# Seven joined pairs of steps for five in the last block of an RWKV and dense kernel, with the late forms ahead of the adds

## The chip, the cores and the metric

One core of a Trainium2 chip runs the kernel. The metric is the device time of one execution in microseconds (us). A core has a matrix engine (TensorE; PE in the profile, its weight loads PEld), a vector engine (VectorE, DVE), a scalar engine (ScalarE, ACT), GpSimd (POOL), and queues for transfers (SP). Each engine runs its own instructions in the order in which they were written and waits for the others by semaphores.

## The reference

An attention block of the RWKV kind runs over 768 tokens of 4 x 8 heads of 48 channels. Its output, 3072 tokens of 384 channels, goes through two dense layers with h - tanh(h) between them.

```python
    for t in range(S):
        kt, vt, rt, wt = (k[:, :, t], v[:, :, t], r[:, :, t], w[:, :, t])
        cur = np.einsum('bhd,bhe->bhde', u[None] * kt, vt)
        y[:, :, t] = np.einsum('bhd,bhde->bhe', rt, state + cur)
        state = wt[:, :, :, None] * state + np.einsum('bhd,bhe->bhde', kt, vt)
...
    h = x @ w_in          # (3072, 384) @ (384, 2048)
    g = h - np.tanh(h)
    return (g @ w_out).astype(np.float32)
```

## The kernel before

**Blocks and steps.** The 3072 tokens are cut into eight blocks of 384 tokens (blocks 0 to 7). While the dense layers of one block run, the attention of the next block is prepared beside them. The dense part of a block has 16 steps f, one for each 128 of the 2048 hidden channels. A plain step (`first`, L885) makes h = w_in[f] x in three matmuls of 384 columns, one for each 128 input channels, in the PSUM bank hp. ScalarE copies h out (L890) and squares it twice (L972, L973), VectorE makes g from it (L893), and ScalarE watches the size of h (L977, "junk").

**The fifteen products.** Two steps make a pair q = f // 2. The second layer of a pair takes 15 products of 128x128 where the plain way takes 18 (class `Fewer`, L1085). Products use g itself or sums of parts of g, the forms of g, which VectorE makes in five additions (`form_g`, L1006). The first two are made right behind g. The other three (numbers 4, 6 and 8) are late: they are kept in `held_back`, then `forming`, and, where steps are joined, `carried`. Products 0 to 11 are added over the pairs in three banks acc in two parts of six: the first part two steps after the pair's last g, the second part one step later. Products 12 to 14, the late products (`others`), are added for four pairs at a time in a scratch bank att. Form 8 is read by the fifth of the second part's six products, which the trace shows as the group `acc<-w_sb,g` behind eight rows of `acc<-forms,g`. At the end of a block ScalarE takes acc out (L1097) and VectorE sums it into the output (`SUMS`, L1120), in the steps of the next block.

**Joined pairs.** Only the last block has no attention to prepare beside it. There the first layer of five of its eight pairs (1 to 5, `TWOS`) is joined too (class `Twos`): two steps by two halves of the tokens by three parts of the input channels, 12 products of 192 columns, are had from 11 (L944). They need sums of weights (`weight_forms`, L916) and of tokens (`token_forms`, L925), made ahead, which lie in tiles that the attention no longer needs (k, r, post). The 11 products go to the two scratch tiles e0 and e1 of two banks each, and to hp. ScalarE copies the first product out (L945), and VectorE makes the two h from it in four adds (L954): the first reads e0, the other three e1.

**Order.** The order of each engine is the order in which the program is written, step by step. For each step the list `ops` sets VectorE's order: `rest` (the products that make g), `formed` (an early form of g), `forming` or `carried` (late ones), `outs` (the four adds), `spare` (sums of the block before, and forms of weights and tokens), `behind` (others). `between` takes two lists in turn. Tiles keep their bank as long as someone reads them; the order of waits shows that a scratch tile att of two banks is handed over as a whole.

**The end.** After pair 5 come four plain steps (12 to 15). Their g goes into the output directly (`added`, L1063), behind a check of the sizes of h.

Of the kernel before, what the change touches and what calls it, by code (L numbers as in the profile page):

```python
# [37 lines left out]
F32 = mybir.dt.float32  # L38
# [13 lines left out]
P = 128  # L52
# [4 lines left out]
NCP = NCH // 2  # L57
NPAIR = H // 2
# [7 lines left out]
DM = H * D  # L66
# [5 lines left out]
HB = NB // 2  # L72
# [3 lines left out]
LAST = 6  # L76
# [37 lines left out]
SUMS = (("sub", (15, 6, 10), (0, 0, 6)), ("sub", (2, 2, 5), (3, 5, 3)),  # L114
        ("add", (6, 7, 13), (1, 7, 1)), ("add", (7, 9, 14), (5, 9, 11)),
        ("sub", (10, 10, 14), (5, 5, 6)), ("add", (11, 12, 11), (10, 2, 10)),
        ("sub", (14, 4, 14), (11, 3, 11)), ("add", (2, 8, 13), (10, 5, 10)),
        ("add", (13, 4, 13), (2, 2, 15)), ("add", (8, 8, 12), (4, 4, 12)),
        ("add", (0, 4, 0), (11, 2, 11)), ("sub", (14, 14, 1)))
PLACES = ((8, 10, 0), (2, 5, 13), (11, 7, 14))  # L120
TWOS = range(1, 6)


SLIGHT = 2.0 ** -6
# [4 lines left out]
def kernel(  # L129
# [170 lines left out]
    def scratch(ps):  # L300
        return ps.tile([P, 2, BANK], F32, name="att", tag="att")
# [594 lines left out]
    class Twos:  # L896
# [3 lines left out]
        def __init__(self):  # L900
            def spare(name):
                return inp.tile([P, 2 * HALF], F32, name=name, tag=name)

            n = (TWOS[-1] + 1 - TWOS[0]) * P
            k, r, post = spare("k"), spare("r"), spare("post")
            self.forms = [t[:, a:a + n].rearrange("p (j c) -> p j c", c=P)
                          for t, a in ((k, 0), (k, n), (r, 0), (r, n), (post, 0))]
            self.turned = [post[:, n + a * HB:n + (a + 1) * HB] for a in range(4)]
            self.to = None

        def weight_forms(self):

            at = w_in_sb[:, 2 * TWOS[0]:2 * TWOS[-1] + 2].rearrange("p (j two) k c -> p j two k c", two=2)
            (a11, a12, a13), (a21, a22, a23) = ([at[:, :, i, k] for k in range(KC)] for i in range(2))
            s1, s2, s3, s4, s5 = self.forms
            return [lambda op=op, of=of: nc.vector.tensor_tensor(out=of[0], in0=of[1], in1=of[2], op=OPS[op])  # L916
                    for op, *of in (("add", s1, a21, a22), ("sub", s3, a11, a21), ("sub", s2, s1, a11),
                                    ("sub", s5, a13, a23), ("sub", s4, a12, s2))]

        def token_forms(self, xs):  # L920

# [6 lines left out]
        def begin(self, ps, j):  # L928

            if self.to is None:  # L930
                self.to = [inp.tile([P, 2 * HALF], F32, name=name, tag=name)[:, 0:8 * HB].rearrange(
                    "p (n t) -> p n t", t=HB) for name in ("pre", "w")]
            h, k = self.to[j % 2], j - TWOS[0]
            e0, e1 = ps.both[(ps.n + 1) % 2], ps.both[ps.n % 2]
            (a11, a12, a13), (_, a22, a23) = ([w_in_sb[:, 2 * j + i, k] for k in range(KC)] for i in range(2))
            s1, s2, s3, s4, s5 = (t[:, k] for t in self.forms)
            t1, t2, t3, t4 = self.turned
            (b11, _), (b21, b22), (b31, b32) = self.first, self.second, self.third
            for to, *of in ((hp[:, 0:HB], (a11, b11)), (e0[:, 0, 0:HB], (a12, b21), (a13, b31)),
                            (e0[:, 0, HB:NB], (s2, t2)), (e1[:, 0, 0:HB], (s3, t3)),  # L940
                            (e1[:, 0, HB:NB], (s1, t1), (a23, b32)), (e1[:, 1, 0:HB], (s4, b22), (s5, b32)),
                            (e1[:, 1, HB:NB], (a22, t4), (a23, b31))):
                for n, (lhs, rhs) in enumerate(of):
                    nc.tensor.matmul(to, lhsT=lhs, rhs=rhs, start=n == 0, stop=n + 1 == len(of))  # L944
            nc.scalar.copy(out=h[:, 7], in_=hp[:, 0:HB])  # L945

            def both(t):
                return t.rearrange("p (n t) -> p n t", t=HB)

            def twice(t):  # L950
                return t.unsqueeze(1).to_broadcast([P, 2, HB])

            self.h = [h[:, n:n + 2].rearrange("p n t -> p (n t)") for n in (0, 2)]
            return [lambda of=of: nc.vector.tensor_tensor(out=of[0], in0=of[1], in1=of[2], op=ALU.add)  # L954
                    for of in ((h[:, 0:5:4], twice(h[:, 7]), both(e0[:, 0, 0:NB])),
                               (h[:, 5:7], twice(h[:, 4]), both(e1[:, 0, 0:NB])),
                               (h[:, 1], h[:, 6], e1[:, 1, 0:HB]),
                               (h[:, 2:4], twice(h[:, 5]), e1[:, 1::-1, HB:NB]))]
# [112 lines left out]
    class Fewer:  # L1071
# [24 lines left out]
        def scaled(self, to, src):  # L1096
            nc.scalar.activation(out=to, in_=src, func=AF.Copy, scale=1.0 / UPSCALE)  # L1097

        def others(self, ps, qs):
            if qs[0] % 4 == 0:  # L1100
                self.apart = scratch(ps)[:, 0]
            for q in qs:
                for n in range(MAIN, len(PRODUCTS)):
                    at = (n - MAIN) * P
                    self.product(self.apart[:, at:at + P], q, n, q % 4 == 0 and n == MAIN,
                                 q in (3, self.pairs - 1))
            if qs[-1] == 3:
                self.half = dense.tile([P, DM], F32, name="o", tag="o", bufs=2)
                self.scaled(self.half, self.apart[:, 0:DM])
# [224 lines left out]
    for i, blk in enumerate(blocks):  # L1334
# [9 lines left out]
        for f in range(NF):  # L1344
# [24 lines left out]
            else:  # L1369
                ahead_of_h, square = [], []  # L1370
            some = ({4: (0, 2), 6: (2, 4), 8: (4, 6), 9: (6, 8), 14: (8, len(SUMS))} if later else
                    {4: (0, 1), 5: (1, 2), 6: (2, 3), 7: (3, 4), 8: (4, 5), 9: (5, 9), 10: (9, 10),
                     11: (10, len(SUMS))}).get(f) if summed else None
            spare = summed[0].sum(*some) if some else []
            if now > 1:
                for of, names in ((later, before.get(f, ())), (after, ahead.get(f, ()))):
# [1 line left out]
                              if of and not name.startswith("bound")]  # L1378
            if i:
                spare += [lambda n=n: form_w(n, 4 if f < 12 else 6, 2) for n in formed_w.get(f, ())]  # L1380
            if i == blocks_n - 2 and f == 13:
                twos = Twos()
            if i == blocks_n - 2 and f in (13, 14):
                spare += twos.weight_forms()[(0, 3)[f - 13]:(3, 5)[f - 13]]
            if not later and f == 1:
                spare += twos.token_forms(here)
            adding = []
            if fewer and second and f > 2 * LAST + 1:
                adding = fewer.sum(*((0, 6) if f % 2 == 0 else (6, len(SUMS))))
            if not now:  # L1390
                ops = square + converting(pieces, 2)
            elif now == 1:
                ops = rest + late + square + converting(pieces, 3)
            elif not i:
                ops = extra + square + (rest + behind + spare if f < 7 else rest[:1] + behind + spare + rest[1:])
            elif outs:
                ops = (between(rest, carried[:1]) + outs[:1] + carried[1:] + formed + outs[1:2] + spare + outs[2:])
                carried = []
            elif joined:
                ops, carried = forming[:1] + between(rest + formed, spare), forming[1:]  # L1400
            elif carried:
                ops, carried = between(rest + formed, carried + behind + spare), []
            elif forming:
                ops = between(rest, forming[:2]) + square + formed + forming[2:]
                ops = (between(ops, behind) if len(behind) > 2 else ops + behind) + spare
            elif adding and f % 2:
                ops = adding[:2] + between(rest, adding[2:3]) + square
                adding = adding[3:]
            elif adding:
                at = n_whole + n_excess  # L1410
                ops = (between(rest, behind) +
                       [lambda: nc.vector.tensor_single_scalar(holds[:, n_whole:at], excess, 0.0, op=ALU.is_le),
                        lambda: sum_held(holds[:, at:at + n_top - 2], top[:, 0:n_top - 2], holds[:, 0:at + n_top - 2],
                                         ends[:, 0:1])] + adding[:4] + square + adding[4:])
            elif square:
                ops = (between(rest, behind) if len(behind) > 2 else rest + behind) + square + formed + extra + spare
            else:
                ops = between(rest + formed, behind + spare)
# [61 lines left out]
                if ins:  # L1480
                    begin_behind(made, ins)
            if f < 2 and summed:
                summed[0].others(ps_a, ((4, 5, 6), (7,))[f])
                if f:
                    behind.append(summed[0].others_summed)
            add_due(now)
# [94 lines left out]
```

## Time and profile before

| what | value |
|---|---|
| median of 3 runs | 544.26 us (542.75 to 544.32) |
| profiled execution | 543.52 us |
| its span, first to last instruction | 541.7 us |
| mean granted TensorE clock | 0.998 |
| last block's first matmul | 471.82 us |
| first matmul of its step 14 | 524.68 us |

The trace is of one execution. A row of the timeline has the start, the time from its start to its last end, the engine, the line and operation, the tiles (out<-in), the shape, and how many instructions of the trace were merged; in brackets stands how long the engine had been idle before, and who released it. A matmul of the program is two rows of the trace. Ends of matmuls are modelled, so the pace of TensorE is read from the start of one group to the start of the next.

### The profile page before, as it was taken

What the parts mean: (1) busy time and instruction counts of PE and PEld (TensorE: products, weight loads), DVE (VectorE), ACT (ScalarE), POOL (GpSimd) and SP (SyncE); (2) the same over time, 40 slices, a digit from 0 to 9 for tenths busy, and PEclk for the clock granted to TensorE, in tenths of its full rate; (3) what the DMA queues carried; (4) which work ended last, traced back from release to release, by engine and by line L of the source; (5) the groups of instructions that cost most, each with busy time, mean ns of one, the idle gap of its engine ahead of it and who ended that gap; (6) DMA issues with size and microseconds to landing.
All of it is one profiled execution on the core that took longest, in us unless ns stands there. A gap on an engine that the chain in (4) does not pass through costs nothing.

```text
span 541.7 us, 15030 instructions
## 1 busy us (share of the span) xinstructions
PE 531.5 (98%) x5750; PEld 410.7 (76%) x5750; DVE 473.4 (87%) x976; ACT 398.4 (74%) x803; POOL 9.2 (2%) x57
## 2 busy tenths in 40 slices
PE   7899999999999999999999999999999999999996
PEld 5656665677877777777877787777878787799974
DVE  7899999999989989789897889879797897859975
ACT  5899986888668876688676887588865886646561
POOL 1100000000000000000000000000000000000001
PEclk9999999999999999999999999999999999999999
DMA  7799732252311632154212532136232320200011
GB/s 276 230 413 328 235 109 88 95 140 64 119 30 68 162 114 61 44 136 131 61 56 73 122 117 67 50 90 161 64 96 60 84 65 2 57 0 1 2 44 47
DMA packets 53048, 56.35 MB, mean 104 GB/s; under 512 B 21488, under 2 KB 50928, under 8 KB 52976
## 3 DMA queue, kind: packets, MB, share of 16 engines
q1 hardware_dynamic: 52592, 55.18, 33.9%
q8 instruction: 49, 0.80, 0.6%
q14 instruction: 23, 0.19, 0.1%
q10 hardware_dynamic: 288, 0.10, 0.1%
q0 software_dynamic: 96, 0.07, 0.1%
HBM read 44.73 MB, written 4.72 MB: 91 GB/s over the span
## 4 chain that ended last, share of the span: by engine, by line
PE 95%; DVE 2%; issue 1%; DMA 0%; PEld 0%; PEldq 0%; DVEq 0%; SPq 0%
PE hp L885 41%; PE acc L1085 27%; PE att L1085 7%; PE acc L1036 5%; PE att L771 4%; PE att L944 3%; PE att L496 2%; PE att L577 1%; PE acc L1063 1%; PE att L885 1%; PE acc L885 1%; DVE post L431 1%; DMA states<-in_wT 0%; DVE scores L504 0%; PE att L681 0%
## 5 line engine op out<-in xcount | busy, mean ns | idle before, releaser
L885 PE MATMUL hp<-xT,w_sb 128*128 128x384 f32 x678 | 238.2, 488 | 0.5 <-DVE w_sb L270 0.5
L885 PEld LDWEIGHTS hp<-xT,w_sb 128*128 128x128 f32 x678 | 121.4, 191 | 64.2 <-issue 0.6
L1085 PE MATMUL acc<-forms,g 128*128 128x128 f32 x972 | 135.8, 276 | 0.0
L1085 PEld LDWEIGHTS acc<-forms,g 128*128 128x128 f32 x972 | 124.3, 192 | 9.3
L890 ACT ACTIVATE h<-hp 128x384 f32<-128x384 f32 x113 | 55.4, 490 | 84.8 <-PE hp L885 84.7
L1006 DVE TENSOR_TENSOR g<-g 128x256 f32<-128x256 f32 x270 | 105.6, 418 | 7.4 <-PE acc L1085 6.5
L893 DVE SCALAR_TENSOR_TENSOR h<-h,s 128x384 f32<-128x384 f32 x118 | 64.9, 550 | 34.6 <-ACT s L972 34.5
L973 ACT ACTIVATE qa<-s,shift 128x384 f32<-128x384 f32 x113 | 69.6, 616 | 3.7
L977 ACT ACTIVATE junk<-s,shift 128x384 bf16<-128x384 f32 x113 | 67.8, 600 | 0.2
L893 DVE SCALAR_TENSOR_TENSOR g<-qa,h 128x384 f32<-128x384 f32 x102 | 56.1, 550 | 1.1
L972 ACT ACTIVATE s<-h 128x384 f32<-128x384 f32 x103 | 53.9, 523 | 3.2
L1085 PEld LDWEIGHTS acc<-w_sb,g 128*128 128x128 f32 x324 | 47.4, 192 | 9.1 <-ACT sums L1053 0.3
L1085 PE MATMUL acc<-w_sb,g 128*128 128x128 f32 x324 | 54.3, 277 | 0.0
L1085 PE MATMUL att<-w_sb,g 128*128 128x128 f32 x216 | 36.2, 275 | 0.0
L1085 PEld LDWEIGHTS att<-w_sb,g 128*128 128x128 f32 x216 | 31.5, 192 | 5.0
L1120 DVE TENSOR_TENSOR sums<-sums 128x256 f32<-128x256 f32 x84 | 33.2, 409 | 2.0 <-ACT sums L1097 1.8
L1036 PE MATMUL acc<-w_sb,sums 128*128 128x384 f32 x96 | 33.7, 487 | 0.0
L266 ACT ACTIVATE up<-raw 128x768 f16<-128x768 f32 (+1 forms) x32 | 33.4, 1080 | 0.0
L1036 PEld LDWEIGHTS acc<-w_sb,sums 128*128 128x128 f32 x96 | 18.0, 190 | 12.3 <-DVE sums L893 0.3
L419 DVE TENSOR_TENSOR_SCAN pre<-w,start 128x780 f32<-128x780 f32 x14 | 25.0, 1782 | 0.8
L431 DVE TENSOR_TENSOR_SCAN post<-w,seed 128x780 f32<-128x780 f32 x14 | 24.8, 1775 | 0.0
L977 ACT ACTIVATION_READ_ACCUMULATOR junk<-s,shift 128x1 f32 x113 | 21.1, 187 | 0.0
(150 smaller groups left out, 600.7 us busy)
## 6 DMA issues: line engine op xcount, KB each, us to landing
raw<-in_weights SPq DMA_DIRECT2D x16, 768.0 KB, 6.9
w<-in_wT SPq DMA_DIRECT2D x7, 780.0 KB, 4.5
k<-in_kT SPq DMA_DIRECT2D x7, 768.0 KB, 4.6
r<-in_rT SPq DMA_DIRECT2D x7, 768.0 KB, 4.6
v_sb<-in_v SPq DMA_DIRECT2D x8, 576.0 KB, 3.9
k<-in_tokens SPq DMA_DIRECT2D x7, 576.0 KB, 4.7
r<-in_tokens SPq DMA_DIRECT2D x7, 576.0 KB, 4.8
out_y<-sums SPq DMA_DIRECT2D x18, 128.0 KB, 1.8
```

The lines of the kernel that those rows point to most:

```text
L266: return lambda: nc.scalar.activation(out=to, in_=of, func=AF.Copy, scale=scale, bias=bias)
L431: return nc.vector.tensor_tensor_scan(out=back(t[:, 0:width]), data0=back(self.tile("w")[:, a:a + width]), data1=back(seed[:, 0:width]), i ...
L885: nc.tensor.matmul(hp, lhsT=w_in_sb[:, f, kc, :], rhs=xT[kc], start=(kc == KC - 1), stop=(kc == 0))
L890: return h, nc.scalar.activation(out=h, in_=hp, func=AF.Copy, scale=1.0 / UPSCALE)
L893: return lambda: nc.vector.scalar_tensor_tensor(out=out, in0=in0, scalar=scalar, in1=in1, op0=op0, op1=ALU.mult)
L972: nc.scalar.activation(out=s, in_=h, func=AF.Square, scale=scale)
L973: nc.scalar.activation(out=qa, in_=s, func=AF.Square, bias=shift[:, 4:5])
L977: nc.scalar.activation(out=junk[:, 0:NB], in_=s, func=AF.Relu, bias=shift[:, 5:6], accum_out=excess[:, at:at + 1])
L1006: return lambda: nc.vector.tensor_tensor(out=G[:, to:to + 2], in0=two(G, g_at(q, a0), g_at(q, a1)), in1=two(G, g_at(q, b0), g_at(q, b1)), ...
L1036: nc.tensor.matmul(acc, lhsT=g[:, j * P:(j + 1) * P], rhs=w_out_sb[:, f, :], start=(f == self.first), stop=(f == NF - 1))
L1085: nc.tensor.matmul(to, lhsT=G[:, g_at(q, a), :], rhs=rhs, start=start, stop=stop, skip_group_check=True)
L1120: ops.append(lambda op=op, at=at: nc.vector.tensor_tensor(out=at[0], in0=at[1], in1=at[2], op=OPS[op]))
```

## The change

It joins all pairs but the last (`TWOS` is now 0 to 6, seven pairs). Steps 0, 1, 12 and 13 of the last block lose their plain matmuls.

With pair 0 joined, its forms are needed sooner. Two of the five weights' forms are made in step 10 of block 6 (they were in step 13), the other three in step 13 (two of them were in step 14), and the tokens' forms in step 14 of block 6 (they were in step 1 of block 7). Two of the longer forms go to the tiles ks and v_sb (`more`).

The first of the 11 products goes to the second bank of e0, no longer to hp. So hp is free, and the late products of block 6 (the changed line calls them by `summed[0]`), which the last block's first two steps add up, go there instead of a scratch tile.

In the steps with adds, all late forms now come ahead of the first add, and the sums of the block before are split around the second add; in step 13, which has no plain step any more, the late forms are put between the products. The sums of steps 10 and 11 are cut at 11 instead of 10.

```diff
-TWOS = range(1, 6)
+TWOS = range(7)
...
-            n = (TWOS[-1] + 1 - TWOS[0]) * P
+            n = len(TWOS) * P
             k, r, post = spare("k"), spare("r"), spare("post")
-            self.forms = [t[:, a:a + n].rearrange("p (j c) -> p j c", c=P)
-                          for t, a in ((k, 0), (k, n), (r, 0), (r, n), (post, 0))]
-            self.turned = [post[:, n + a * HB:n + (a + 1) * HB] for a in range(4)]
+            self.forms = [t[:, 0:n].rearrange("p (j c) -> p j c", c=P) for t in (k, r, post)]
+            self.turned = [t[:, n + a * HB:n + (a + 1) * HB] for t in (k, r) for a in range(2)]
...
+        def more(self):
+            n = len(TWOS) * P
+            ks = work.tile([P, NPAIR * NCP * P], F32, name="ks", tag="ks", bufs=1)
+            v_sb = inp.tile([P, NCP * DM], F32, name="v_sb", tag="v_sb")
+            self.forms += [t[:, 0:n].rearrange("p (j c) -> p j c", c=P) for t in (ks, v_sb)]
...
-            for to, *of in ((hp[:, 0:HB], (a11, b11)), (e0[:, 0, 0:HB], (a12, b21), (a13, b31)),
+            for to, *of in ((e0[:, 1, 0:HB], (a11, b11)), (e0[:, 0, 0:HB], (a12, b21), (a13, b31)),
...
-            nc.scalar.copy(out=h[:, 7], in_=hp[:, 0:HB])
+            nc.scalar.copy(out=h[:, 7], in_=e0[:, 1, 0:HB])
...
-        def others(self, ps, qs):
+        def others(self, ps, qs, to=None):
             if qs[0] % 4 == 0:
-                self.apart = scratch(ps)[:, 0]
+                self.apart = scratch(ps)[:, 0] if to is None else to
...
-                    {4: (0, 1), 5: (1, 2), 6: (2, 3), 7: (3, 4), 8: (4, 5), 9: (5, 9), 10: (9, 10),
-                     11: (10, len(SUMS))}).get(f) if summed else None
+                    {4: (0, 1), 5: (1, 2), 6: (2, 3), 7: (3, 4), 8: (4, 5), 9: (5, 9), 10: (9, 11),
+                     11: (11, len(SUMS))}).get(f) if summed else None
...
-            if i == blocks_n - 2 and f == 13:
-                twos = Twos()
-            if i == blocks_n - 2 and f in (13, 14):
-                spare += twos.weight_forms()[(0, 3)[f - 13]:(3, 5)[f - 13]]
-            if not later and f == 1:
-                spare += twos.token_forms(here)
+            if i == blocks_n - 2:
+                if f == 10:
+                    twos = Twos()
+                    spare += twos.weight_forms(False)
+                elif f == 13:
+                    twos.more()
+                    spare += twos.weight_forms(True)
+                elif f == 14:
+                    spare += twos.token_forms(xT)
...
             elif outs:
-                ops = (between(rest, carried[:1]) + outs[:1] + carried[1:] + formed + outs[1:2] + spare + outs[2:])
+                ops = (between(rest, carried) + outs[:1] + formed + spare[:-1] + outs[1:2] + spare[-1:] + outs[2:])
                 carried = []
+            elif joined and f < 2 * LAST:
+                ops, carried = forming[:1] + between(rest + formed, spare), forming[1:]
             elif joined:
-                ops, carried = forming[:1] + between(rest + formed, spare), forming[1:]
+                ops = forming[:1] + between(rest, forming[1:])
...
-                summed[0].others(ps_a, ((4, 5, 6), (7,))[f])
+                summed[0].others(ps_a, ((4, 5, 6), (7,))[f], None if later else hp)
```

Three places show how instructions move. The first is TensorE at the start of the last block; xT_5114 to xT_5116 are its input, att_124 and att_125 the scratch tiles, acc_130 and acc_601 two of the three banks acc. Before:

```order
L885 MATMUL hp<-xT_5116,w_sb 128x384
L885 MATMUL hp<-xT_5115,w_sb 128x384
L885 MATMUL hp<-xT_5114,w_sb 128x384
L1085 MATMUL att_124<-w_sb,g 128x128
L1085 MATMUL att_124<-forms,g 128x128
L1085 MATMUL att_124<-w_sb,g 128x128 x2
```

Now, at the same place:

```order
L949 MATMUL att_124<-xT_5114,w_sb 128x192
L949 MATMUL att_124<-xT_5115,w_sb 128x192
L949 MATMUL att_124<-xT_5116,w_sb 128x192
L949 MATMUL att_124<-k,r 128x192
L949 MATMUL att_125<-r,post 128x192
L949 MATMUL att_125<-k 128x192
L949 MATMUL att_125<-xT_5116,w_sb 128x192
L949 MATMUL att_125<-xT_5115,ks 128x192
L949 MATMUL att_125<-xT_5116,v_sb 128x192
L949 MATMUL att_125<-r,w_sb 128x192
L949 MATMUL att_125<-xT_5116,w_sb 128x192
```

The eleven products of pair 0 stand where step 0 stood; the late products follow further on, in hp, and step 1 is gone. The first product is now in e0 (att_124).

The second place is VectorE between two joined pairs of the last block (pair 1's second h and pair 2's first add); the brackets say which engines an instruction waits for. Before:

```order
L893 SCALAR_TENSOR_TENSOR w<-w,s 128x384 [waits Activation_49]
L1006 TENSOR_TENSOR g<-g 128x256 [waits PE_49]
L893 SCALAR_TENSOR_TENSOR g<-qa,w 128x384 [waits DVE_49,Activation_49]
L954 TENSOR_TENSOR pre<-pre,att_125 128x2x192 [waits PE_49,Activation_49]
L1006 TENSOR_TENSOR g<-g 128x256 [waits DVE_49] x2
L954 TENSOR_TENSOR pre<-pre,att_124 128x384 [waits DVE_49,PE_49]
```

Now:

```order
L893 SCALAR_TENSOR_TENSOR w<-w,s 128x384 [waits Activation_49]
L1011 TENSOR_TENSOR g<-g 128x256 [waits PE_49]
L893 SCALAR_TENSOR_TENSOR g<-qa,w 128x384 [waits DVE_49,Activation_49]
L1011 TENSOR_TENSOR g<-g 128x256 [waits DVE_49,PE_49]
L959 TENSOR_TENSOR pre<-pre,att_124 128x2x192 [waits Activation_49]
L1011 TENSOR_TENSOR g<-g 128x256 [waits DVE_49]
L959 TENSOR_TENSOR pre<-pre,att_125 128x384 [waits DVE_49,PE_49]
```

One of the two forms behind the first add (form 8) stands ahead of it, and that add waits for ScalarE alone.

The third place is VectorE in step 10 of block 6, behind the masks of the next attention. Now:

```order
L399 COPY_PREDICATED scores<-mask_all,diagonal 128x2x384
L893 SCALAR_TENSOR_TENSOR h<-h,s 128x384
L921 TENSOR_TENSOR k<-w_sb 128x896
L893 SCALAR_TENSOR_TENSOR g<-qa,h 128x384
L921 TENSOR_TENSOR r<-k,w_sb 128x896
L1011 TENSOR_TENSOR g<-g 128x256
```

Before, the same rows stood there without the two of L921, which are the first two weights' forms; they were in step 13, as rows of 640.

More of the change, by code (lines that the diff above doesn't have):

```diff
@@ L902, in spare, with weight_forms @@
                 return inp.tile([P, 2 * HALF], F32, name=name, tag=name)
-            n = (TWOS[-1] + 1 - TWOS[0]) * P
+            n = len(TWOS) * P
             k, r, post = spare("k"), spare("r"), spare("post")
-            self.forms = [t[:, a:a + n].rearrange("p (j c) -> p j c", c=P)
-                          for t, a in ((k, 0), (k, n), (r, 0), (r, n), (post, 0))]
-            self.turned = [post[:, n + a * HB:n + (a + 1) * HB] for a in range(4)]
+            self.forms = [t[:, 0:n].rearrange("p (j c) -> p j c", c=P) for t in (k, r, post)]
+            self.turned = [t[:, n + a * HB:n + (a + 1) * HB] for t in (k, r) for a in range(2)]
             self.to = None
-        def weight_forms(self):
+        def more(self):
[3 more added lines that the diff above has]
+            self.forms += [t[:, 0:n].rearrange("p (j c) -> p j c", c=P) for t in (ks, v_sb)]
+        def weight_forms(self, late):
             at = w_in_sb[:, 2 * TWOS[0]:2 * TWOS[-1] + 2].rearrange("p (j two) k c -> p j two k c", two=2)
             (a11, a12, a13), (a21, a22, a23) = ([at[:, :, i, k] for k in range(KC)] for i in range(2))
-            s1, s2, s3, s4, s5 = self.forms
+            s1, s2, s3, s4, s5 = self.forms if late else self.forms + [None] * 2
             return [lambda op=op, of=of: nc.vector.tensor_tensor(out=of[0], in0=of[1], in1=of[2], op=OPS[op])
-                    for op, *of in (("add", s1, a21, a22), ("sub", s3, a11, a21), ("sub", s2, s1, a11),
-                                    ("sub", s5, a13, a23), ("sub", s4, a12, s2))]
+                    for op, *of in (("add", s1, a21, a22), ("sub", s2, s1, a11), ("sub", s3, a11, a21),
+                                    ("sub", s4, a12, s2), ("sub", s5, a13, a23))[2 if late else 0:5 if late else 2]]
         def token_forms(self, xs):
```

## The prediction, made before the change was run

> **What bounds the kernel now.** I read the page first, then busy time by stretches, then TensorE's timeline from 455 us to the end, and last what VectorE and ScalarE do beside it. In this fence the first two lines are the page's (busy time; shares of the chain of waits), the other two are stretches of the last block.
>
> ```profile
> PE 531.5 (98%) x5750; PEld 410.7 (76%) x5750; DVE 473.4 (87%) x976; ACT 398.4 (74%) x803; POOL 9.2 (2%) x57
> PE 95%; DVE 2%; issue 1%; DMA 0%; PEld 0%; PEldq 0%; DVEq 0%; SPq 0%
> ...
> 480.00:485.00 5.00, 5.00 (x37) 5.00 (x37) 2.55 (x6) 2.19 (x6) 0.00 (x0) 1.00 0.00 0
> ...
> 505.00:510.00 5.00, 5.00 (x45) 5.00 (x44) 4.96 (x14) 4.17 (x10) 0.00 (x0) 1.00 0.02 5
> ```
>
> TensorE is on 95% of the chain, so the change can only save what it takes out of TensorE's row of work or out of its waits. The columns of a stretch are TensorE, weight loads, VectorE, ScalarE: in the last block VectorE goes from half idle (2.55 of 5) to full (4.96 of 5). That is the engine whose lateness could eat the gain. A busy TensorE is only modelled, so its waits are read from the starts of its groups. Each matmul of the program is two rows in the trace.
>
> ```profile
> 471.82 2.10 PE L885 MATMUL hp<-xT,w_sb 128*128 128x384 f32 x6
> 473.76 0.39 PE L1085 MATMUL att<-w_sb,g 128*128 128x128 f32 x2
> ...
> 481.06 0.49 PE L944 MATMUL hp<-xT,w_sb 128*128 128x192 f32 x2
> ...
> 482.36 0.49 PE L944 MATMUL att<-post,r 128*128 128x192 f32 x2
> ...
> 484.63 1.05 PE L1085 MATMUL acc<-forms,g 128*128 128x128 f32 x8
> 485.52 0.39 PE L1085 MATMUL acc<-w_sb,g 128*128 128x128 f32 x2
> ```
>
> A plain step (three matmuls of 384 columns) takes 473.76 - 471.82 = 1.94 us. A joined pair (eleven of 192 columns) takes 484.63 - 481.06 = 3.57 us. Its first four products, those in e0 after the change, take 482.36 - 481.06 = 1.30 us. A row of 128 columns takes (485.52 - 484.63) / 8 = 0.111 us.
>
> **The change part by part.** *Two more joined pairs.* They take out four plain steps, 4 x 1.94 = 7.76, and put in two pairs, 2 x 3.57 = 7.14: TensorE has **0.6 us** less to do. Everything else on TensorE keeps its count; block 7's fifteen-product groups only stand behind other work, and its late ones go into hp.
>
> The Trainium skill speaks against smaller matmuls ("Larger matmuls are more efficient than smaller matmuls, when possible", Perfetto Trace Analysis, section Optimizing Tensor Performance). The trace agrees, but weakly: were a 192-column matmul exactly half of a 384-column one, a pair would take 22 x 0.161 = 3.55 us and the two would save 0.66, not 0.6.
>
> *Late forms first.* TensorE waits in two places of this stretch. Rows of TensorE and VectorE:
>
> ```profile
> 490.95 1.05 PE L1085 MATMUL acc<-forms,g 128*128 128x128 f32 x8
> 491.89 0.49 PE L1085 MATMUL acc<-w_sb,g 128*128 128x128 f32 x2
> 492.22 0.39 PE L1085 MATMUL acc<-forms,g 128*128 128x128 f32 x2
> ...
> 497.36 1.05 PE L1085 MATMUL acc<-forms,g 128*128 128x128 f32 x8
> 498.25 0.39 PE L1085 MATMUL acc<-w_sb,g 128*128 128x128 f32 x2
> ...
> 517.16 1.05 PE L1085 MATMUL acc<-forms,g 128*128 128x128 f32 x8
> 518.18 0.49 PE L1085 MATMUL acc<-w_sb,g 128*128 128x128 f32 x2
> 518.50 0.39 PE L1085 MATMUL acc<-forms,g 128*128 128x128 f32 x2
> ...
> 491.42 0.75 DVE L1006 TENSOR_TENSOR g<-g 128x256 f32<-128x256 f32 x2
> ...
> 497.55 0.76 DVE L1006 TENSOR_TENSOR g<-g 128x256 f32<-128x256 f32 x2
> ...
> 517.70 0.76 DVE L1006 TENSOR_TENSOR g<-g 128x256 f32<-128x256 f32 x2
> ```
>
> Eight rows are 0.89 us, so the next group could start at 491.84 and 518.05; it starts at 491.89 and 518.18, and its two rows then take 0.33 and 0.32 instead of 0.22. That is 0.16 + 0.23 = **0.39 us** of waiting. The group reads the last form, the first of VectorE's two g<-g (0.42 us alone): ready at 491.84 and about 518.1, just when TensorE asks. In the middle case it is ready at 497.97 for 498.25, so 0.3 us of room. The change puts this form ahead of the pair's first add. At the first place that is a gap: VectorE stands still there until the copy has landed.
>
> ```profile
> 490.10 0.55 DVE L893 SCALAR_TENSOR_TENSOR g<-qa,w 128x384 f32<-128x384 f32 x1
> 490.95 0.55 DVE L954 TENSOR_TENSOR pre<-pre,att 128x384 f32<-128x384 f32 x1 [0.30 <-ACT pre L945]
> ```
>
> So the form moves from 491.42 to about 490.6 and the wait at 491.84 is gone. At 518 the place itself changes: pair 6 stands between, so TensorE asks 3.57 - 1.94 = 1.63 us later relative to the step's beginning. I take all 0.39; the bounds are 0 (the wait comes back elsewhere) and 0.39.
>
> *The first product moves from hp into e0.* ScalarE's copy of it now has to wait for all of e0 (in the new order the add behind the copy waits for ScalarE alone, no longer for TensorE too).
>
> ```profile
> 481.92 0.30 ACT L945 COPY w<-hp 128x192 f32<-128x192 f32 x1
> ...
> 482.63 0.55 DVE L954 TENSOR_TENSOR w<-w,att 128x384 f32<-128x384 f32 x1 [1.03 <-PE att L944]
> ...
> 484.83 1.41 DVE L954 TENSOR_TENSOR w<-w,att 128x384 f32<-128x384 f32 x3 [1.32 <-PE att L944]
> ```
>
> Before, the copy ran while e0 filled and the add came 0.27 us behind e0's end (482.36). Now copy and add follow each other: e0's end + 0.27 + 0.30, so the add is 0.3 us later. The second add waits for the end of the pair anyway (484.83, 0.2 behind 484.63), with 1.32 us idle ahead of it. Cost 0, up to 0.3 a pair if that cover were gone.
>
> *The weights' forms.* Seven pairs make each form 896 elements instead of 640, and two of the five go to step 10 of block 6.
>
> ```profile
> 431.60 1.35 DVE L384 TENSOR_TENSOR k<-k,u_row 128x1152 f32<-128x1152 f32 x1
> ...
> 450.95 0.56 DVE L893 SCALAR_TENSOR_TENSOR h<-h,s 128x384 f32<-128x384 f32 x1 [2.47 <-ACT s L972]
> ...
> 456.55 0.36 DVE L589 TENSOR_TENSOR states<-states,whole 128x192 f32<-128x192 f32 x1
> ...
> 459.06 1.56 PE L771 MATMUL att<-pre,states 48*48 48x64 f32 x96
> ...
> 461.20 0.82 DVE L916 TENSOR_TENSOR k<-w_sb 128x640 f32<-128x640 f32 x1
> ...
> 465.21 0.56 DVE L893 SCALAR_TENSOR_TENSOR h<-h,s 128x384 f32<-128x384 f32 x1 [1.73 <-ACT s L972]
> ```
>
> 640 elements take 0.82, 1152 take 1.35: 896 lies at 1.08. The two early ones, 2.2 us at most, fall into the 2.47 us in which VectorE waits for ScalarE before 450.95. Were that cover gone, the states would come up to 2.2 us later than 456.9, and TensorE asks for them at 459.06: room of 2.15 more. The three at step 13 add 3 x 0.26 = 0.8 us ahead of an idle time of 1.73. Cost 0.
>
> *The tokens' forms* move from step 1 of the last block to step 14 of block 6, behind the sums, where the last holes of xT have just been sent.
>
> ```profile
> L791 SPq DMA_DIRECT2D xT<-late x6: 527/560/582, 462.9 to 466.0; - x6
> ...
> DMA to landing us min/median/max: 1.8/1.9/3.3
> ...
> 467.70 0.82 DVE L916 TENSOR_TENSOR post<-w_sb 128x640 f32<-128x640 f32 x1
> ...
> 469.17 0.55 DVE L893 SCALAR_TENSOR_TENSOR h<-h,s 128x384 f32<-128x384 f32 x1
> ...
> 475.04 0.56 DVE L893 SCALAR_TENSOR_TENSOR h<-h,s 128x384 f32<-128x384 f32 x1 [1.60 <-ACT s L972]
> ```
>
> The last hole is sent at 466.0 and lands between 467.8 and 469.3; the four forms of 192 elements (1.3 us at most, under 0.35 each) stand where two weight forms stood from 467.70 to 469.17. VectorE's queue behind them, the g of steps 14 and 15, is up to 469.3 + 1.3 - 469.17 = 1.4 us late. TensorE asks for the forms made of them after pair 0, at 471.82 + 3.57 = 475.4, and VectorE had 1.60 us to spare before 475.04. Cost 0.
>
> **The sum:** 0.6 + 0.39 = **1.0 us**, all ahead of the last two steps, which keep their own chain. The profiled execution took 543.52 us (span 541.7), so 542.5 by it. That execution lies 0.74 below the median of the runs shown, 544.26, and above their lowest, 542.75; from the median the sum gives 543.3. I take the middle, **542.9 us**, 0.18% off. A measurement of this kernel tells about 0.3% (1.6 us) from no change, so the likeliest verdict is no change.
>
> **Rivals.** *Thin room in slower executions (faster by about 1.7 us).* The profiled execution is a good one. With 0.3 us of room for the form at 498.25, a VectorE that runs 0.3 us later makes TensorE wait at every pair. If the 0.74 us between this execution and the median are such waits, the change ends them too: 0.6 + 0.39 + 0.74 = 1.7 us, 542.5 from the median. For it: VectorE at 4.96 of 5. Against: nothing shows where the 0.74 us lie.
>
> *The matmuls alone (0.6 us, or less).* The waits of 0.39 come back in other places, since VectorE now has four more adds in each of two further pairs, and no idle time at 505 to 510. Then 543.3, as the mean of 542.9 and 543.7. Against it: pair 0's adds come ahead of the half idle stretch at 480 to 485, and pair 6, which ends near 518.3, has its adds done near 518.3 + 0.2 + 1.41 = 519.9, while TensorE asks for the next late forms only behind three groups of twelve rows, 3 x 12 x 0.111 = 4.0 us after the pair.
>
> *The bank given up (slower).* The copy that waits for all of e0 holds the first add, this holds VectorE's queue, and the h and g behind it reach TensorE late. Where ScalarE is free, at pairs 0, 1, 5 and 6, the copy loses the 0.97 us of three products. If all of it reached TensorE: 4 x 0.97 - 1.0 = 2.9 us slower, 546.8 from 543.9, the middle of the profiled execution and the median. It decides only once the first add ends later than the pair itself less the form between them: 3.57 - 0.5 - 0.4 = 2.7 us after the pair's start, and by the rows above it begins 1.9 us after it. The Trainium skill backs this rival: it asks that independent groups "rotate through different PSUM banks" so that emptying one overlaps the next (Perfetto Trace Analysis, section Optimizing Tensor Performance), and the change gives up a bank. Against the rival stand the 1.32 us that VectorE idles before the second add.
>
> **Chances.** All of the sum, 1.0 us: 0.58. Thin room, 1.7 us: 0.22. Matmuls alone: 0.13. Slower: 0.07. By the spread of the three runs (1.6 us) the sum's case reads as faster one time in five (0.12), and thin room, which lies at the bound, seven times in ten (0.15): faster 0.28 with a little of the third. Slower by over 0.3%: 0.06. Within: 0.66. The range goes from thin room read low, 541.2, to the matmuls alone read high, 544.3.
>
> **What would show it.** Right: seven groups of L949 of 3.57 us, and the rows of the plain steps L885 down by 24. The plain step 14 of the last block starts 1.0 us earlier than here:
>
> ```profile
> 524.68 2.10 PE L885 MATMUL hp<-xT,w_sb 128*128 128x384 f32 x6
> ```
>
> No group of two behind eight takes 0.33. VectorE waits for the holes of xT at about 467.7 and TensorE does not notice. Wrong: TensorE waiting before a group of acc in the last block by more than 0.2 us; h at 450.95 or the states later; the first add of a pair more than 2.7 us behind its start; or the step-14 start moved by under 0.5 or over 1.5 us.

## The result, and the profile after

| what | before | after |
|---|---|---|
| median of 22 runs each | 543.06 us (541.91 to 544.41) | 542.33 us (541.08 to 543.71) |
| ratio after to before, 95% interval | | 0.9981 (0.9972 to 0.9989) |
| profiled execution | 543.52 us | 541.15 us |
| its span | 541.7 us | 539.4 us |
| first plain matmul into hp | 28.6 us | 27.3 us |
| the middle: last block's first matmul to that of its step 14 | 52.86 us | 51.89 us |

The whole interval of the ratio lies under the bound of 0.3%, so this counts as no change, as forecast (542.9 us, likeliest verdict "within"). The interval, 0.6 to 1.5 us of 543, is still on the faster side of 1 and holds the forecast gain of 1.0 us. What whole runs hardly resolve, the profile does: below, "the middle" is the last row of the table.

From the profile page of the changed kernel, busy time and chain of waits:

```profile
PE 530.7 (98%) x5770; PEld 413.0 (77%) x5770; DVE 477.9 (89%) x984; ACT 397.5 (74%) x801; POOL 9.2 (2%) x57
PE 95%; DVE 2%; DMA 1%; issue 1%; SPq 0%; DVEq 0%
```

TensorE is as full as before, with 0.8 us less of busy time; VectorE has 8 instructions more (four more adds in each of two pairs) and ScalarE 2 fewer. The timeline of TensorE: the first matmul of step 9 of block 6, then the last block from its start.

```profile
440.40 0.81 PE L885 MATMUL hp<-xT,w_sb 128*128 128x384 f32 x2
...
470.45 1.14 PE L949 MATMUL att<-xT,w_sb 128*128 128x192 f32 x6
471.43 0.49 PE L949 MATMUL att<-k,r 128*128 128x192 f32 x2
...
474.03 1.05 PE L1090 MATMUL acc<-forms,g 128*128 128x128 f32 x8
...
479.39 0.82 PE L949 MATMUL att<-xT,w_sb 128*128 128x192 f32 x4
...
489.28 1.05 PE L1090 MATMUL acc<-forms,g 128*128 128x128 f32 x8
490.17 0.39 PE L1090 MATMUL acc<-w_sb,g 128*128 128x128 f32 x2
490.39 0.39 PE L1090 MATMUL acc<-forms,g 128*128 128x128 f32 x2
...
516.98 1.05 PE L1090 MATMUL acc<-forms,g 128*128 128x128 f32 x8
517.87 0.39 PE L1090 MATMUL acc<-w_sb,g 128*128 128x128 f32 x2
518.09 0.39 PE L1090 MATMUL acc<-forms,g 128*128 128x128 f32 x2
...
522.34 1.13 PE L885 MATMUL hp<-xT,w_sb 128*128 128x384 f32 x3
```

Pair 0 takes 474.03 - 470.45 = 3.58 us. At both places where TensorE waited, eight rows now take 0.89 us and the next two 0.22: no wait. The middle is 522.34 - 470.45 = 51.89 us, 0.97 less than 524.68 - 471.82.

The two profiled executions differ by 2.37 us, so 1.4 us more than the middle gives. Where nearly all of those lie shows in the rows of the plain matmuls (count; shortest, median, longest in ns; first and last start), of before and of after:

```profile
L885 PE MATMUL hp<-xT,w_sb x678: 485/486/591, 28.6 to 530.2; 128*128 128x384 f32 x170
```

```profile
L885 PE MATMUL hp<-xT,w_sb x654: 486/486/590, 27.3 to 527.8; 128*128 128x384 f32 x164
```

From before to after the count fell by 24 rows, the four plain steps. The first plain matmul into hp starts 1.3 us sooner: nearly all the rest of the difference lies ahead of all that the change touches. One place of it is a stop of TensorE for which the profile names no other engine ("issue"), in before and in after:

```profile
21.39 0.50 PE L496 MATMUL att<-pre,post 48*64 48x64 f32 x18 [1.54 <-issue]
```

```profile
19.85 0.50 PE L496 MATMUL att<-pre,post 48*64 48x64 f32 x18 [0.26 <-issue]
```

VectorE of the changed kernel, at the places that the prediction costed at nothing, at pair 2 (488.90 and 489.28) and at pair 5 (from 509.81):

```profile
447.38 1.08 DVE L921 TENSOR_TENSOR r<-k,w_sb 128x896 f32<-128x896 f32 x1
...
449.57 0.56 DVE L893 SCALAR_TENSOR_TENSOR h<-h,s 128x384 f32<-128x384 f32 x1 [0.78 <-ACT s L977]
...
467.49 0.36 DVE L930 TENSOR_TENSOR k<-xT 128x192 f32<-128x192 f32 x1 [1.08 <-DMA xT<-late]
...
481.24 0.56 DVE L959 TENSOR_TENSOR w<-w,att 128x384 f32<-128x384 f32 x1 [0.83 <-ACT w L950]
...
483.17 1.41 DVE L959 TENSOR_TENSOR w<-w,att 128x384 f32<-128x384 f32 x3 [1.03 <-PE att L949]
...
488.90 0.42 DVE L1011 TENSOR_TENSOR g<-g 128x256 f32<-128x256 f32 x1
...
489.28 0.55 DVE L959 TENSOR_TENSOR pre<-pre,att 128x384 f32<-128x384 f32 x1
...
509.81 0.42 DVE L1125 TENSOR_TENSOR sums<-sums 128x256 f32<-128x256 f32 x1
510.93 0.55 DVE L959 TENSOR_TENSOR w<-w,att 128x384 f32<-128x384 f32 x1 [0.70 <-PE att L949]
```

The weights' form of 896 elements takes 1.08 us, as estimated, and 0.78 of the 2.47 us of idle time is left behind the two of them. The tokens' forms wait for the last holes of xT until 467.49, and TensorE goes on. At pair 1 the second add (483.17) still waits for the end of the pair. At pair 2 form 8 starts at 488.90, ahead of the first add, and is ready at 489.32, while TensorE asks for it at 490.17.

### The profile page after: what moved, and what is told of

Its sections match the earlier page's. It is cut to its first block, busy times and chain, and to the rows that moved or that the text cites. A ratio compares the mean times of both kernels' runs of the same rounds, so it can differ in the third digit from the quotient of the medians.

```text
span 539.4 us, 15067 instructions
## 1 busy us (share of the span) xinstructions
PE 530.7 (98%) x5770; PEld 413.0 (77%) x5770; DVE 477.9 (89%) x984; ACT 397.5 (74%) x801; POOL 9.2 (2%) x57
## 4 chain that ended last, share of the span: by engine, by line
PE 95%; DVE 2%; DMA 1%; issue 1%; SPq 0%; DVEq 0%
PE hp L885 39%; PE acc L1090 27%; PE att L1090 6%; PE acc L1041 5%; PE att L949 5%; PE att L771 4%; PE att L496 2%; PE att L577 1%; PE acc L1068 1%; PE att L885 1%; DMA r<-in_rT 1%; PE acc L885 1%; DVE pre L419 1%; PE hp L1090 0%; PE att L681 0%
## 5 line engine op out<-in xcount | busy, mean ns | idle before, releaser
L885 PE MATMUL hp<-xT,w_sb 128*128 128x384 f32 x654 | 229.8, 487 | 0.5 <-DVE w_sb L270 0.5
L885 PEld LDWEIGHTS hp<-xT,w_sb 128*128 128x128 f32 x654 | 116.9, 190 | 62.3 <-issue 0.6
L890 ACT ACTIVATE h<-hp 128x384 f32<-128x384 f32 x109 | 53.5, 491 | 79.3 <-PE hp L885 79.3
L893 DVE SCALAR_TENSOR_TENSOR h<-h,s 128x384 f32<-128x384 f32 x114 | 62.8, 551 | 28.6 <-ACT s L977 28.5
L893 DVE SCALAR_TENSOR_TENSOR g<-qa,h 128x384 f32<-128x384 f32 x98 | 54.0, 551 | 0.8
L977 ACT ACTIVATE s<-h 128x384 f32<-128x384 f32 x99 | 51.8, 523 | 3.1
L1090 PE MATMUL att<-w_sb,g 128*128 128x128 f32 x200 | 33.4, 275 | 0.0
L1090 PEld LDWEIGHTS att<-w_sb,g 128*128 128x128 f32 x200 | 29.0, 192 | 4.2
```

Source lines behind the costliest of these rows:

```text
L885: nc.tensor.matmul(hp, lhsT=w_in_sb[:, f, kc, :], rhs=xT[kc], start=(kc == KC - 1), stop=(kc == 0))
L890: return h, nc.scalar.activation(out=h, in_=hp, func=AF.Copy, scale=1.0 / UPSCALE)
L893: return lambda: nc.vector.scalar_tensor_tensor(out=out, in0=in0, scalar=scalar, in1=in1, op0=op0, op1=ALU.mult)
L977: nc.scalar.activation(out=s, in_=h, func=AF.Square, scale=scale)
L1090: nc.tensor.matmul(to, lhsT=G[:, g_at(q, a), :], rhs=rhs, start=start, stop=stop, skip_group_check=True)
```

## The experiments

Eleven kernels ran, once each with a profile. Besides the middle, "the approach" is the stretch from the first matmul of step 9 of block 6 to the last block's first matmul, 30.05 us in both kernels (after: 470.45 - 440.40). Between two executions whose code is the same up to a place, these stretches differ by 0.02 us or less. The whole times scatter more, and most of that is the first plain matmul: the whole time less the three other columns leaves 431.9 to 432.2 us, and 432.5 in tokens_step13.

| kernel (all in us) | whole time | first plain matmul | approach | middle |
|---|---|---|---|---|
| before | 543.52 | 28.6 | 30.05 | 52.86 |
| after | 541.15 | 27.3 | 30.05 | 51.89 |
| late_first_alone | 542.37 | 27.6 | 30.05 | 52.69 |
| forms_behind_add | 543.37 | 29.4 | 30.05 | 52.04 |
| pairs_0_to_5 | 544.08 | 29.7 | 30.05 | 52.18 |
| first_in_hp | 543.27 | 29.1 | 30.05 | 51.89 |
| pairs_1_to_6 | 542.00 | 27.7 | 30.05 | 52.18 |
| early_forms_twice | 543.35 | 29.5 | 30.05 | 51.88 |
| early_forms_thrice | 542.63 | 27.2 | 31.38 | 51.88 |
| tokens_step13 | 547.92 | 27.9 | 34.44 | 53.07 |
| sums_cut_old | 541.81 | 28.0 | 30.05 | 51.89 |
| pairs_0_to_5_cut_old | 541.96 | 27.5 | 30.04 | 52.41 |
| late_first_and_sums | 542.30 | 27.7 | 30.05 | 52.48 |

### The order of the late forms, alone and undone

late_first_alone is the kernel before with one line:

```diff
-ops = (between(rest, carried[:1]) + outs[:1] + carried[1:] + formed + outs[1:2] + spare + outs[2:])
+ops = (between(rest, carried) + outs[:1] + formed + spare[:-1] + outs[1:2] + spare[-1:] + outs[2:])
```

> The kernel before, with one part of the change alone: the late forms ahead of a pair's first add. 'The middle' is the stretch from the last block's first matmul to the first matmul of its step 14; it took 52.86 us before and 51.89 in the changed kernel. My theory: the wait of 0.16 us behind pair 2's eight rows ends, the 0.23 us near 518 stay, since that place is behind pair 5 and plain step 12, which the order does not touch: middle 52.70. Rival (the waits only wander, since VectorE has no slack): 52.86, with the 0.16 us at another group. Rival (the order alone ends both): 52.47.

TensorE's timeline of it at the two places:

```profile
489.94 1.05 PE L1085 MATMUL acc<-forms,g 128*128 128x128 f32 x8
490.83 0.39 PE L1085 MATMUL acc<-w_sb,g 128*128 128x128 f32 x2
491.05 0.39 PE L1085 MATMUL acc<-forms,g 128*128 128x128 f32 x2
...
516.00 1.05 PE L1085 MATMUL acc<-forms,g 128*128 128x128 f32 x8
517.01 0.49 PE L1085 MATMUL acc<-w_sb,g 128*128 128x128 f32 x2
517.34 0.39 PE L1085 MATMUL acc<-forms,g 128*128 128x128 f32 x2
```

At pair 2 the wait is gone; near 517 eight rows still take 1.01 us and the two behind them 0.33. The middle is 52.69: the order is worth 0.17 us, at one place only.

forms_behind_add is the changed kernel with the old order of those forms.

```diff
-ops = (between(rest, carried) + outs[:1] + formed + spare[:-1] + outs[1:2] + spare[-1:] + outs[2:])
+ops = (between(rest, carried[:1]) + outs[:1] + carried[1:] + formed + spare[:-1] + outs[1:2] +
+       spare[-1:] + outs[2:])
```

> The changed kernel, with the old order of the late forms: one ahead of the first add, form 8 and its fellow behind it. My theory: form 8 then starts about 489.83 and is ready at 490.25, while TensorE asks for it at 490.17, so a wait of 0.1 to 0.25 us comes back behind pair 2's eight rows, and none near 517.9, where pair 6 now stands between: middle 52.0 to 52.15 against 51.89. Rival (the order is worth nothing, the waits were ended by the pairs and the bank): 51.89. Rival (the order ended both): 52.28.

```profile
491.40 1.05 PE L1090 MATMUL acc<-forms,g 128*128 128x128 f32 x8
492.35 0.49 PE L1090 MATMUL acc<-w_sb,g 128*128 128x128 f32 x2
492.68 0.39 PE L1090 MATMUL acc<-forms,g 128*128 128x128 f32 x2
```

Its TensorE waits again behind pair 2's eight rows (0.95 for 0.89, then 0.33 for 0.22), and the middle is 52.04, 0.15 longer. So alone and undone agree on this term.

### What ended the wait near 518

pairs_0_to_5 leaves pair 6 as two plain steps, with the rest of the change in place.

```diff
-TWOS = range(7)
+TWOS = range(6)
```

> The changed kernel with six joined pairs, 0 to 5: pair 6 goes back to two plain steps, all else stays. My theory: pair 6's 0.31 us of matmuls come back (2 x 1.94 less 3.57), and, since that place is what ended it, the wait of 0.23 us near 518 too: middle 52.2 plus 0.23 = 52.43. Rival (the new order ended that wait): 52.20.

The middle is 52.18. The matmuls of one pair come back (0.29 of 0.31 us), the wait does not. My reason for the 0.23 us, pair 6 in that place, falls as the only one; but the new order alone did not end that wait either. VectorE's rows at pair 5 of this kernel showed a part of the change that the prediction had passed over, the cut of the sums of block 6:

```profile
512.21 0.42 DVE L1125 TENSOR_TENSOR sums<-sums 128x256 f32<-128x256 f32 x1
513.33 0.56 DVE L959 TENSOR_TENSOR w<-w,att 128x384 f32<-128x384 f32 x1 [0.70 <-PE att L949]
513.80 0.42 DVE L1125 TENSOR_TENSOR sums<-sums 128x256 f32<-128x256 f32 x1
```

One sum more stands in step 10, ahead of the second add, in time in which VectorE waits for TensorE anyway; it was in step 11, among the instructions ahead of the late forms. It comes ahead of that add because the new order also splits the sums around the add; with the old cut, step 10 has a single sum, and that one stays behind the add. Three kernels test this. sums_cut_old is the changed kernel with the old cut, pairs_0_to_5_cut_old the same with six pairs, and late_first_and_sums the kernel before with the new order and the new cut.

```diff
-{4: (0, 1), 5: (1, 2), 6: (2, 3), 7: (3, 4), 8: (4, 5), 9: (5, 9), 10: (9, 11),
- 11: (11, len(SUMS))}).get(f) if summed else None
+{4: (0, 1), 5: (1, 2), 6: (2, 3), 7: (3, 4), 8: (4, 5), 9: (5, 9), 10: (9, 10),
+ 11: (10, len(SUMS))}).get(f) if summed else None
```

> The changed kernel with the sums of block 6 cut as before (one sum of 256 columns goes back from step 10 to step 11 of the last block). Pairs 0 to 5 alone (without pair 6) showed no wait near 518 and the new order alone did, so neither of them ended it alone. New theory: VectorE's sum of 0.33 us, taken out from between pair 5's last add and the late forms and put into VectorE's idle time before pair 5's second add, ended it. With pair 6 in its place TensorE asks 1.63 us later and so this kernel still has no wait (pair 6 would have ended it too): middle 51.88. Rival (the sum alone ends it, pair 6 does not help, because its first add stands ahead of the late form): middle 52.0 to 52.2, with a wait before the group of two behind eight rows near 517.9.

> Six joined pairs, 0 to 5, with the sums cut as before. New theory: the wait of 0.23 us near 518 is back: middle 52.19 + 0.23 = 52.42. Rival (pair 0 joined, or the first product in e0, ended it): 52.19.

> The kernel before with two parts of the change alone: the late forms ahead of the first add, and the sums cut at 11. New theory: both waits are gone without any further pair: middle 52.86 - 0.16 - 0.23 = 52.47. Rival (the sums' cut needs the other parts): 52.70.

VectorE and TensorE of pairs_0_to_5_cut_old:

```profile
511.24 0.56 DVE L959 TENSOR_TENSOR w<-w,att 128x384 f32<-128x384 f32 x1 [1.03 <-PE att L949]
511.71 0.42 DVE L1125 TENSOR_TENSOR sums<-sums 128x256 f32<-128x256 f32 x1
...
513.58 0.42 DVE L1125 TENSOR_TENSOR sums<-sums 128x256 f32<-128x256 f32 x1
```

```profile
515.65 1.05 PE L1090 MATMUL acc<-forms,g 128*128 128x128 f32 x8
516.66 0.49 PE L1090 MATMUL acc<-w_sb,g 128*128 128x128 f32 x2
516.99 0.39 PE L1090 MATMUL acc<-forms,g 128*128 128x128 f32 x2
```

With the sum back in step 11 VectorE idles 1.03 instead of 0.70 us ahead of the second add, and the wait is back (1.01 for 0.89, then 0.33): 52.41. late_first_and_sums has 52.48 without any further pair, 0.21 under late_first_alone. sums_cut_old has 51.89 and no wait there (eight rows in 0.89 us, the next two in 0.22): with pair 6 the old cut costs nothing. So, with the new order in place in all these kernels, either the further pair or the cut of the sums ends this wait by itself, and the changed kernel has both. The new cut without the split was not run.

### The bank, and pair 0

first_in_hp puts the first product of pairs 1 to 6 into hp again.

```diff
-for to, *of in ((e0[:, 1, 0:HB], (a11, b11)),
+alone = hp[:, 0:HB] if j else e0[:, 1, 0:HB]
+for to, *of in ((alone, (a11, b11)),
...
-nc.scalar.copy(out=h[:, 7], in_=e0[:, 1, 0:HB])
+nc.scalar.copy(out=h[:, 7], in_=alone)
```

> The changed kernel with the first product of pairs 1 to 6 in hp again (pair 0 stays in e0, since hp holds the late products then). My theory: ScalarE copies it while e0 fills, the first add of pairs 1, 5 and 6 starts up to 0.3 us earlier (1.55 instead of 1.85 us behind the pair's start), the second add still ends no sooner than the pair, TensorE notices nothing: middle 51.89 within 0.05. Rival (the given-up bank costs TensorE something): middle shorter by up to 0.3 us a pair, 51.6 to 50.1.

TensorE and then VectorE of this kernel at pair 1:

```profile
481.23 0.49 PE L950 MATMUL hp<-xT,w_sb 128*128 128x192 f32 x2
```

```profile
482.80 0.55 DVE L960 TENSOR_TENSOR w<-w,att 128x384 f32<-128x384 f32 x1 [0.55 <-PE att L950]
...
485.01 1.41 DVE L960 TENSOR_TENSOR w<-w,att 128x384 f32<-128x384 f32 x3 [1.31 <-PE att L950]
```

The first add starts 1.57 us behind the pair's start (after: 481.24 - 479.39 = 1.85), the second 3.78 behind it in both kernels. The 0.28 us end in VectorE's wait for the end of the pair: 1.31 us here, 1.03 in the changed kernel. The middle is the same to 0.01. Giving up the bank at pairs 1 to 6 costs nothing here.

pairs_1_to_6 takes pair 0 out instead and leaves the late products of block 6 in a scratch tile.

```diff
-TWOS = range(7)
+TWOS = range(1, 7)
...
-summed[0].others(ps_a, ((4, 5, 6), (7,))[f], None if later else hp)
+summed[0].others(ps_a, ((4, 5, 6), (7,))[f])
```

> The changed kernel with six joined pairs, 1 to 6: pair 0 goes back to two plain steps and the late products of block 6 to a scratch tile; all else stays. My theory: only the matmuls of one pair come back (0.31 us), no wait: middle 52.20. Rival (pair 0 joined has a price of its own, late forms or the bank): shorter than 52.10. Rival (pair 0 joined or hp for the late products ended a wait): longer than 52.30.

The middle is 52.18, so pair 0 is worth its matmuls, and no price of its own shows; nor does one for the place of the late products. Pair 7, which is left to plain steps ahead of the kernel's end, was not tried.

### The cover of the forms

early_forms_twice and early_forms_thrice make the two early weights' forms two and three times over, with the same values.

```diff
     twos = Twos()
     spare += twos.weight_forms(False)
+    spare += twos.weight_forms(False)
```

> The changed kernel with the two early weights' forms of step 10 of block 6 made twice over (four operations of 896 elements instead of two, 1.08 us each, 2.16 us more for VectorE). 'The approach' is the stretch from the first matmul of step 9 of block 6 to the last block's first matmul, 30.05 us in both kernels. My theory: 0.78 us go into VectorE's idle time that is left before 449.57, the other 1.38 us make the states late by that, and TensorE asks for them only 2.15 us after they are done: approach 30.05 still. Rival (the cover was only just enough, or another group asks sooner): 0.8 to 2.2 us more, 30.9 to 32.2.

> The changed kernel with the two early weights' forms made three times over (4.32 us more for VectorE). My theory: 4.32 less 0.78 of idle time less 2.15 of room before the states are used at 457.69 is 1.4 us, less up to 0.6 that small gaps between the sums of states give back: TensorE waits 0.8 to 1.4 us ahead of the matmuls on states, approach 30.85 to 31.45. Rival (VectorE's half of the time free hides this too): 30.05. Rival (no cover at all): 34.4.

Twice over, the approach stays at 30.05. Three times over it is 31.38, 1.33 more for 4.3 us of added work. TensorE of that kernel ahead of the attention's matmuls on states:

```profile
458.00 0.31 PE L771 MATMUL att<-pre,states 48*48 48x64 f32 x2 [0.32 <-DVE states L589]
458.79 1.67 PE L771 MATMUL att<-pre,states 48*48 48x64 f32 x91 [0.47 <-DVE states L589]
```

The wait is where the room was computed to end: for the states, and nowhere else in the approach. The times in brackets are shorter than the loss, since ends of matmuls are modelled. By starts, TensorE comes to the states 0.39 us later behind the group ahead than in the changed kernel, and from there to the next plain step it takes 0.94 us longer (461.78 - 458.00 against 460.53 - 457.69): together the 1.33. The cover was idle time plus room ahead of the next user, and both count.

tokens_step13 makes the tokens' forms one step sooner.

```diff
-    spare += twos.weight_forms(True)
-elif f == 14:
-    spare += twos.token_forms(xT)
+    spare += twos.token_forms(xT) + twos.weight_forms(True)
```

> The changed kernel with the tokens' forms in step 13 of block 6 ahead of the three weights' forms, so before the last holes of xT have landed. My theory: VectorE stands still from about 459.8 until the last hole has landed (about 467.5), and all its queue is up to 8 us late; the h and g of steps 13 to 15 and pair 0's forms come late, and TensorE waits for them near the start of the last block: approach and middle together longer by 3 to 6 us. Rival (VectorE's idle time at 470 to 485 hides it): no longer, by less than 0.3 us.

VectorE, then TensorE of this kernel:

```profile
468.53 0.36 DVE L930 TENSOR_TENSOR k<-xT 128x192 f32<-128x192 f32 x1 [7.62 <-DMA xT<-late]
```

```profile
474.83 1.23 PE L1090 MATMUL acc<-forms,g 128*128 128x128 f32 x4 [3.66 <-DVE g L1011]
475.84 2.13 PE L949 MATMUL att<-xT,w_sb 128*128 128x192 f32 x6
477.76 0.73 PE L949 MATMUL att<-k,r 128*128 128x192 f32 x2
```

VectorE stands still for 7.62 us, and 3.66 us of that reach TensorE. Approach and middle together are 34.44 + 53.07 - 30.05 - 51.89 = 5.57 us longer; the last section says where the part beyond the stall comes from. The same four forms cost nothing one step later, where VectorE waits 1.08 us for the same transfer.

## Why the prediction was right, point by point

- **Matmuls, 0.6 us: right.** Six pairs cost 0.29 us more than seven, whichever of the two is left out (52.18 against 51.89), so 0.58 for both. The aside on smaller matmuls has a small slip: half of a row of 384 columns is 1.94 / 12 = 0.162 us, not 0.161, so the saving would be 0.65 us against the 0.62 of the rows, a difference near the rounding.
- **Waits, 0.39 us: right in size, half right in cause.** The order is worth 0.17 us at pair 2, as argued. Near 518 the step "At 518 the place itself changes: pair 6 stands between" names a sufficient cause, but the cut of the sums, which the prediction left out, is another, and the kernel would have lost that wait with six pairs too. That the 0.23 us came out whole is in part luck: the reason given was not the only one at work. Order and cut together give 0.38 us in the kernel before without one joined pair more (52.86 - 52.48).
- **The sum:** 1.0 forecast, 0.97 in the middle, and the ratio's interval gives 0.6 to 1.5.
- **Costs at nothing: right.** At pair 1, copy and add in e0 came 1.85 us behind the pair's start (1.9 forecast), the forms of 896 took 1.08, and the approach is 30.05 in both kernels. The thrice-made forms and the tokens' forms a step sooner show that both covers had an end, the first at about 3 us of work on top of the change: 4.3 added, 1.33 seen.
- **One sign of being wrong was badly chosen.** A first add more than 2.7 us behind its pair's start does occur: 3.58 us at pair 2 (489.28 - 485.70), 3.34 and 3.09 at pairs 3 and 4. The kernel before had 3.58, 3.30 and 3.17 at the same pairs. VectorE and ScalarE are still at earlier work there, and the idle time ahead of the second add, which the prediction read at pair 1, does not exist at these three pairs. TensorE still does not wait behind these pairs in the changed kernel, so this lag alone says nothing of TensorE's time.
- **Thin room in slower executions: false.** Executions that began late have the same middle as those that began early: 51.88 with the first plain matmul at 29.5 and at 27.2 us, and 52.18 with six pairs at 29.7 and at 27.7. The gain by whole runs, 0.6 to 1.5 us, leaves out this rival's 1.7 too. No second execution of before was profiled, so where its 0.74 us to the median lie was not seen; in the executions that were, such differences stand for the most part ahead of the first plain matmul.
- **The matmuls alone: false.** One wait of 0.06 us, ahead of pair 2, is left in the middle, and it was there before.
- **The bank given up: false.** The Trainium skill's advice to rotate through banks (Perfetto Trace Analysis, section Optimizing Tensor Performance) brings nothing here: with the bank back at pairs 1 to 6 the middle is unchanged.
- **The absolute time:** 0.57 us high. The sum was set against the middle of one execution and a median of three; the median of 22 runs before is 543.06, which less 0.97 is 542.1, 0.2 us from the measured median.

## What to carry to other kernels

An instruction of an engine that is late for another can be moved into the time in which that engine already waits, and one sum of 0.42 us put there, with the late forms already ahead of the adds, was worth 0.2 us, not much less than a joined pair (0.3). Before a wait is put down to one part of a change, each part that touches the late engine's order has to be listed: two of them can each be enough, and then undoing one shows nothing. Where whole runs scatter by more than the effect, measure it as the stretch between two matmuls of the same execution; here that resolved 0.02 us under a scatter of 2.5.

## What the runs showed of the hardware that was not expected

In tokens_step13 the stall of TensorE cost more than its length. Busy times by stretches (TensorE, weight loads, VectorE, ScalarE, GpSimd; then the granted clock):

```profile
471.00:474.50 3.50, 0.17 (x2) 0.00 (x0) 3.50 (x7) 1.57 (x4) 0.00 (x0) 1.00 0.00 0
474.50:475.50 1.00, 0.67 (x3) 0.68 (x4) 1.00 (x4) 0.00 (x0) 0.00 (x0) 0.67 0.09 27
475.50:478.00 2.50, 2.50 (x10) 2.50 (x10) 2.50 (x7) 0.00 (x0) 0.00 (x0) 0.50 0.57 173
478.00:480.00 2.00, 2.00 (x13) 2.00 (x13) 1.51 (x4) 0.32 (x1) 0.00 (x0) 0.94 0.21 65
480.00:482.00 2.00, 2.00 (x18) 2.00 (x17) 1.16 (x3) 0.22 (x1) 0.00 (x0) 1.00 0.00 0
```

After 3.66 us without work the granted clock was 0.50 from 474.83 to about 478.2, some 3.4 us (0.67 and 0.94 are the means of stretches that hold the two changes of clock). The four rows at 474.83 took 1.01 us, up to 475.84, where four of them take 0.45 at full speed, so 0.56 more. Six rows of pair 0 took 1.92 us (475.84 to 477.76) instead of 0.98 (470.45 to 471.43 in the changed kernel), and the middle was 53.07 - 51.89 = 1.18 us longer, with the same instructions. So the lower clock cost about 1.7 of the 5.57 us; the other 3.8 are the stall, taken from start to start. The waits of 0.32 and 0.47 us in early_forms_thrice left it at full speed (middle 51.88). The Trainium skill states the rule (TensorE: Matmul & The Clock Gate, section Why this matters for your kernels): gaps without matmuls of more than about 3 us bring the half clock back. This trace agrees, with 3.66 us; where the limit lies between 0.47 and 3.66 us, no run here shows.
